# Attention with a SoLU layer on one core: small steps of three engines given out one by one

## Chip, cores and metric

The kernel runs on one core of one Trainium2 chip. The metric is device time in microseconds (us), the median of several runs. An engine is named as in the profile: PE is TensorE (matmuls), PEld its weight loads, DVE is VectorE, ACT is ScalarE, POOL is GpSimd, SP issues the DMAs.

## What is computed

For 8 batches of 8 heads, 576 positions and 64 columns per head, causal attention with a decay that is a running sum of log f; then a layer on the 4608 rows of 512 columns that come out: a product with w_in (512 x 1024), SoLU, a layer norm over 1024 columns and a product with w_out (1024 x 512).

```python
scores = scale * np.matmul(q, k.transpose(0, 1, 3, 2))
cum = np.cumsum(np.log(np.clip(f, 0.0001, 1.0)), axis=-1)
scores = np.where(causal, -1e9, scores + cum[:, :, :, None] - cum[:, :, None, :])
attn = np.exp(scores - np.max(scores, axis=-1, keepdims=True))
attn = attn / (np.sum(attn, axis=-1, keepdims=True) + 1e-09)
x = np.matmul(attn, v)                    # then heads side by side: (4608, 512)
h = x @ w_in
e = np.exp(h - np.max(h, axis=-1, keepdims=True))
solu = h * (e / (np.sum(e, axis=-1, keepdims=True) + 1e-09))
ln = (solu - mu) / np.sqrt(var + 1e-06) * g_ln
out = ln @ w_out
```

## The kernel before

**Pairs.** Attention goes by pairs of heads: 8 batches of 4 pairs. A pair's 576 queries are cut into five tiles (64, 128, 128, 128, 128 rows), and tile i sees 64 + 128 i keys. Per tile and head: PE makes the scores in a PSUM bank (lines 847, and 843 or 845 for the decay); one DVE instruction adds the mask, finds the extreme of a row and, for the larger tiles, writes the scores to SBUF (L868); ACT takes the exponential with its row sums (L873); a column step on POOL turns the sums into what is inverted (L879, tile `sm`), DVE inverts it (L880, `ri`). Then a scaled copy makes the float16 upper half of the probabilities (`copied`, printed as L527 when ACT does it and as L529 for DVE or POOL; tiles `p16s` and `wo_p`), and DVE makes the lower half (L901). A transposing DMA turns them, and PE multiplies with the values (L947). A copy out of PSUM makes the upper half of x (L962, `x_h`), DVE the lower half (L963).

**The first batch** is exact: its probabilities are scaled in float32 in place (L529, tile `p`, on POOL), turned on PE (L920), copied out of PSUM (`t_p`), and multiplied in float32 (L942).

**Layer.** Every 128 rows of x are one of 36 layer steps: product with w_in (L987, into `hps`), row maximum on DVE (L996), exponential on ACT (L998), weighing on DVE (L1002), sum of squares on ACT (L1010), five column steps on POOL (L1005 to L1007, L1013, L1014, tile `st`), normalising on POOL (L1018, tile `e`), an upper half (ACT, L527, `z<-e`), a lower half (POOL, L1023), a transposing DMA, product with w_out (L1052), a scaled copy out of PSUM on ACT (L1084, `y`), and the DMA out. Every product in float16 is three: upper by upper, upper by lower, lower by upper. PE runs them as two halves of 64 columns side by side where the order permits.

**Preparation.** w_in and w_out are read as pairs of words, put together on ACT, POOL and DVE (L608 to L644), and scaled by powers of two that come from their largest value: DVE finds it per row (L651, `top_wi`), PE turns the column (L667), DVE makes the factor, and PE spreads it over the partitions (L692). The same is done per batch for q, k and v (tiles `top`, `scale`); there ACT's squares (L709) give the size.

**Order.** The order of all engines is written out: `Plan.op` records an operation with its engine, its planned duration `ns`, what it reads and writes, and whether it uses the SBUF port that DVE and POOL share (`port`); the tuple `ORDER` gives the numbers of the 3766 operations, and `schedule` deals them out to the engines in that order, with planned start times. From these planned times comes one thing more: where the plan leaves PE idle for over 200 ns in the first 60 us, lines 1173 to 1178 put in matmuls on the identity that write into a free PSUM bank and are read by nobody ("fillers" here; 0.85 of the idle time up to 13.5 us, 0.75 up to 60 us, constant `FILLED`).

## Time and profile before

| | |
|---|---|
| three runs | 634.25, 632.65, 632.1 us; median 632.65 us |
| profiled execution | 632.48 us, of which 630.8 us span from first to last instruction |
| PE busy | 614.6 us (97%), 7852 instructions |
| DVE busy | 540.5 us (86%), 1647 instructions |
| ACT busy | 513.4 us (81%), 1295 instructions |
| POOL busy | 415.1 us (66%), 663 instructions |
| granted TensorE clock, mean | 1.000 |

A busy engine is one that has an instruction under way. A matmul's own duration contains its way through the array, so two matmuls that follow each other overlap in the table of rows; how fast PE goes is read from start to start. An idle time in brackets stands before the row that it precedes, with what ended it.

### The profile page before, as it was taken

The numbers are of one execution on the slowest core, as the hardware profiler recorded it, in microseconds if no ns is written. First come the engines' busy times: TensorE is split into PE (matmuls) and PEld (weight loads), VectorE is DVE, ScalarE is ACT, GpSimd is POOL, SyncE is SP. The second block draws the span as 40 slices with busy tenths as digits, with TensorE's granted clock in tenths as the row PEclk, the third lists the DMA queues.
The fourth block names the chain that finished last, engine by engine and source line by source line (L and its number), as shares of the span: only waits on it lengthen the run. The fifth ranks groups of instructions, "written<-read, shape, count | busy, mean of one in ns | idle before, by whom it ended". The sixth has DMA issues, their size and how long they took to land.

```text
span 630.8 us, 20471 instructions
## 1 busy us (share of the span) xinstructions
PE 614.6 (97%) x7852; PEld 362.5 (57%) x7852; DVE 540.5 (86%) x1647; ACT 513.4 (81%) x1295; POOL 415.1 (66%) x663
## 2 busy tenths in 40 slices
PE   5899999999999999999999999999999999999997
PEld 4566665565555656556565655565655655655555
DVE  6888999999999999999999998999999888774321
ACT  6798979989988997989999888899797878765342
POOL 6786761576868745878679868674777753748440
PEclk9999999999999999999999999999999999999999
DMA  8846318989999999999999999899798884876641
GB/s 331 290 153 261 122 58 178 198 165 222 205 169 190 174 230 163 214 152 254 181 201 157 257 178 261 172 169 211 126 146 149 138 167 86 155 132 126 131 118 50
DMA packets 262722, 110.99 MB, mean 176 GB/s; under 512 B 248288, under 2 KB 248736, under 8 KB 261600
## 3 DMA queue, kind: packets, MB, share of 16 engines
q1 hardware_dynamic: 262624, 109.69, 84.1%
q8 instruction: 61, 1.00, 0.7%
q14 instruction: 37, 0.30, 0.1%
HBM read 38.27 MB, written 9.66 MB: 76 GB/s over the span
## 4 chain that ended last, share of the span: by engine, by line
PE 78%; DVE 10%; DMA 5%; ACT 4%; issue 2%; POOL 2%; SPq 1%; DVEq 0%; POOLq 0%; ACTq 0%
PE ps L1052 26%; PE hps L987 25%; PE ps L847 10%; PE ps L947 10%; PE ps L845 3%; DVE p L868 2%; DMA wo_raw<-in_w_in_dram 2%; PE ps L920 1%; DMA zz<-z 1%; DVE wo_p L901 1%; DVE st L996 1%; DVE p16s L901 1%; DMA t_p<-wo_p 1%; PE ps L942 1%; DMA t_raw<-in_w_out_dram 1%
## 5 line engine op out<-in xcount | busy, mean ns | idle before, releaser
L1052 PE MATMUL ps<-wo_f,zz 128*64 128x512 f16 (+1 forms) x1599 | 196.2, 380 | 0.6 <-DMA zz<-z 0.6
L873 ACT ACTIVATE p<-p,nm 128x320 f32<-128x320 f32 (+4 forms) x208 | 133.0, 641 | 13.3 <-DVE nm L868 12.1
L1052 PEld LDWEIGHTS <-zz 128*64 128x64 f16 (+1 forms) x1599 | 90.5, 109 | 84.5 <-issue 7.1
L987 PE MATMUL hps<-wi_h,x_h 128*64 128x512 f16 (+1 forms) x564 | 111.4, 383 | 0.2
L987 PE MATMUL hps<-wi_l,x_h 128*64 128x512 f16 (+1 forms) x564 | 110.2, 379 | 0.0
L987 PE MATMUL hps<-wi_h,x_l 128*64 128x512 f16 (+1 forms) x564 | 110.2, 379 | 0.0
L868 DVE CUSTOM_DVE_ANT_0 p<-ps,mask 128x320 f32<-128x320 f32 (+3 forms) x208 | 99.5, 496 | 6.7 <-PE ps L920 2.4
L847 PE MATMUL ps<-qk 64*128 64x288 f16 (+9 forms) x1056 | 100.7, 303 | 1.8 <-DMA qk<-in_qk_dram 1.0
L879 POOL TENSOR_SCALAR sm<-sm 128x2 f32<-128x2 f32 (+1 forms) x128 | 39.7, 310 | 85.0 <-ACT p L873 53.1
L987 PEld LDWEIGHTS <-x_h 128*64 128x64 f16 (+1 forms) x1128 | 59.8, 109 | 59.1 <-issue 14.7
L1023 POOL TENSOR_TENSOR z<-e,z 128x512 f16<-128x512 f32 x64 | 77.2, 1220 | 24.7 <-ACT z L527 23.9
L901 DVE SCALAR_TENSOR_TENSOR wo_p<-p,ri,wo_p 128x448 f16<-128x448 f32 (+1 forms) x112 | 85.5, 778 | 7.5 <-ACT wo_p L527 6.8
L947 PEld LDWEIGHTS <-v 128*64 128x64 f16 x2520 | 72.8, 110 | 10.5 <-issue 2.7
L947 PE MATMUL ps<-t_p,v 128*64 128x128 f16 (+1 forms) x2520 | 76.3, 218 | 0.1
L996 DVE TENSOR_REDUCE st<-hps 128x1 f32<-128x1024 f32 x36 | 43.8, 1216 | 18.8 <-PE hps L987 18.6
L529 POOL TENSOR_SCALAR wo_p<-p,ri 128x576 f16<-128x576 f32 x56 | 46.5, 834 | 11.3 <-DVE ri L880 9.7
L998 ACT ACTIVATE e<-hps,st,unscale 128x1024 f32<-128x1024 f32 x32 | 38.4, 1201 | 16.2 <-DVE st L997 12.4
L1002 DVE SCALAR_TENSOR_TENSOR e<-hps,e 128x1024 f32<-128x1024 f32 x36 | 43.7, 1214 | 9.0 <-ACT e L998 8.8
L847 PEld LDWEIGHTS <-qk 64*128 64x128 f16 x864 | 32.4, 94 | 32.4 <-issue 21.6
L845 PE MATMUL ps<-crow,pick 64*128 64x448 bf16 (+1 forms) x360 | 50.9, 276 | 0.0
L1010 ACT ACTIVATE junk<-e,st 128x1024 bf16<-128x1024 f32 x36 | 41.2, 1145 | 11.6 <-DVE e L1002 10.0
L987 PEld LDWEIGHTS <-x_l 128*64 128x64 f16 (+1 forms) x564 | 32.6, 110 | 29.6
(188 smaller groups left out, 1176.7 us busy)
## 6 DMA issues: line engine op xcount, KB each, us to landing
raws<-in_qk_dram SPq DMA_DIRECT2D x24, 576.0 KB, 5.8
vraw<-in_v_dram SPq DMA_DIRECT2D x8, 1280.0 KB, 7.1
out_dram<-y SPq DMA_DIRECT2D x35, 256.0 KB, 3.2
qk<-in_qk_dram SPq DMA_DIRECT2D x8, 576.0 KB, 6.4
wo_raw<-in_w_in_dram SPq DMA_DIRECT2D x4, 1024.0 KB, 8.6
vraw<-in_w_out_dram SPq DMA_DIRECT2D x2, 1024.0 KB, 4.9
t_raw<-in_w_out_dram SPq DMA_DIRECT2D x2, 1024.0 KB, 5.0
t_p<-p16s SPq DMA_TRANSPOSE x84, 3.5
```

What stands on the lines that cost most here:

```text
L529: (nc.vector if eng == DVE else nc.gpsimd).tensor_scalar(now(out_), now(in_), scale, by, ALU.mult, ALU.mult)
L845: nc.tensor.matmul(dst, pick[row(h), a2, a1:a1 + 1].broadcast_to([D, P]), crow[row(h), a2, cols], start=False, stop=True)
L847: nc.tensor.matmul(dst, x[row(h), 0, q0:q0 + P], y[row(h), 1, cols], start=(n == 0), stop=False)
L868: op(DVE, R_NS[i] if n == 0 else 442, at[i][h] + STEPS[0], lambda i=i, h=h, n=n, a=a, e=e, x=x, m0=m0: nc.vector.tensor_tensor_reduce(home ...
L873: op(ACT, E_NS[i] + (0 if banked(p, i) or i == 4 else 28), at[i][h] + STEPS[1], lambda i=i, h=h, x=x: nc.scalar.activation(home(i, h), hom ...
L901: op(DVE, L_NS[j], at[j][g] + STEPS[4], lambda j=j, g=g, nq=nq, h16=h16, l16=l16, r1=r1: nc.vector.scalar_tensor_tensor(l16(), home(j, g, ...
L947: nc.tensor.matmul(o[row(h), a:a + n], v16[m][:, x, 2 * j + h], t[:, y, i + j if h else i - j], start=(j == 0 and c == 0), stop=(j == i an ...
L987: nc.tensor.matmul(hps[k, sl], x[:, k], w[:, c, sl], start=start, stop=stop)
L996: op(DVE, 1215, at, lambda: nc.vector.tensor_reduce(s[:, 0:1], hps, axis=AX.X, op=ALU.max, negate=True), [("h",)], [("st", n % 2)])
L1002: nc.vector.scalar_tensor_tensor(et, hps, 1.0 / DFF, et, ALU.mult, ALU.mult, accum_out=s[:, 3:4])
L1023: op(POOL, 1085, at, lambda a=a: nc.gpsimd.tensor_tensor(z16[:, a, 1], e2[:, a], z16[:, a, 0], ALU.subtract), [ek, zk_], [(*zk_, "l", a)])
L1052: nc.tensor.matmul(y[t], zz[:, a, x, j][:, t], wo(w, k), start=(k == 0 and n == 0), stop=(k == NFC - 1 and n == 2))
```

## The change

Operations that could run on several engines are no longer bound by class. `Plan.op` takes `either`, a table of engines with planned durations, and looks its own number up in a new table `ON`: 83 numbers for ACT, 151 for DVE, 57 for POOL; an operation that is in none keeps the engine of its class. The tuple `ORDER` is a new permutation of the same 3766 numbers. No other constant differs.

```diff
+        o.either, o.may = either, port
+        if either:
+            eng, given = next((e for e in either if len(self.ops) in ON.get(e, ())), eng), fn
+            ns, port = either[eng], port and eng == DVE
+
+            def fn():
+                given(o.eng)
...
+ON = {
+    ACT: {
+        83, 91, 92, 113, 128, 129, 181, 217, 380, 384, 416, 420, 422, 424, 440, 450, 452, 454, 456, 460, 490, 492, 496, 652, 1040, 1103, 1113, 1115,
...
     def copied(eng, ns, due, out_, in_, reads, writes, scale=1.0, clear=(), port=True, by=1.0):
 
-        def fn():
-            if eng == ACT:
+        def fn(e):
+            if e == ACT:
                 nc.scalar.activation(now(out_), now(in_), AF.Copy, scale=scale)
             else:
-                (nc.vector if eng == DVE else nc.gpsimd).tensor_scalar(now(out_), now(in_), scale, by, ALU.mult, ALU.mult)
-        op(eng, ns[eng], due, fn, reads, writes, clear=clear, port=port and eng == DVE)
+                engine(e).tensor_scalar(now(out_), now(in_), scale, by, ALU.mult, ALU.mult)
+        either = ns if by == 1.0 else {e: x for e, x in ns.items() if e != ACT}
+        op(eng, ns[eng], due, fn, reads, writes, clear=clear, port=port, either=either)
...
-        op(POOL, 310, at[i][1] + STEPS[2], lambda: nc.gpsimd.tensor_scalar(sums, sums, 1.0e-9, 1.0 / P_UP, ALU.add, ALU.mult), sk, [("se", m, i)])
+        op(POOL, 310, at[i][1] + STEPS[2], lambda e: engine(e).tensor_scalar(sums, sums, 1.0e-9, 1.0 if p < NFP * NPAIR else 1.0 / P_UP, ALU.add, ALU.mult), sk, [("se", m, i)], port=True, either={POOL: 310, DVE: 67})
...
-                copied(P_SCALE[j], {POOL: N_NS[j], ACT: 187 + 0.83 * w, DVE: 67 + 0.6 * w}, at[j][g] + STEPS[3], *[lambda j=j, g=g, nq=nq: home(j, g, nq)] * 2,
-                       [("ri", m, j), ("p", j)], [("p", j, g)], scale=ri[m][:nq, j, g:g + 1], by=1.0 / P_UP)
+                copied(P_SCALE[j], {POOL: N_NS[j], ACT: 187 + 0.83 * w, DVE: 117 + 0.6 * w}, at[j][g] + STEPS[3], *[lambda j=j, g=g, nq=nq: home(j, g, nq)] * 2,
+                       [("ri", m, j), ("p", j)], [("p", j, g)], scale=ri[m][:nq, j, g:g + 1])
...
-            op(ACT, 68 + 0.83 * w, at + XSTEP[0], lambda xo=xo, key=key, w=w: nc.scalar.activation(xo[0], ps[plan.place[key]][:, :w], AF.Copy, scale=up), [key, *uk], xk)
+            copied(ACT, {ACT: 68 + 0.83 * w, DVE: (122 if exact else 72) + 1.05 * w}, at + XSTEP[0], xo[0], lambda key=key, w=w: ps[plan.place[key]][:, :w], [key, *uk], xk, scale=up, port=False)
```

In the same way `either` is given to two memsets, two steps of the running sum, the backwards copy of it, the upper half of v, four of the layer's five column steps, the normalising, the lower half of z and the copy of y. For the first batch the factor 1 / P_UP is no longer taken in both the column step and the scaling, so that ACT, which multiplies by one factor, can do the scaling too.

Counted in the built programs, by kind (before, then now):

| kind | before | now |
|---|---|---|
| column step on the sums (`sm`) | POOL 128 | POOL 92, DVE 36 |
| column steps of the layer (`st`; L1005, L1006, L1007, L1013) | POOL 144 | POOL 105, DVE 39 |
| scaling of the first batch's `p` | POOL 40 | POOL 23, ACT 9, DVE 8 |
| upper half of the probabilities, larger tiles (`wo_p`) | ACT 56, POOL 56 | ACT 58, POOL 50, DVE 4 |
| the same, 320 columns, from SBUF (`p16s`) | ACT 56 | ACT 29, POOL 23, DVE 4 |
| the same, from PSUM, 64 and 192 columns (`p16s`) | ACT 112 | ACT 93, DVE 19 |
| `x_h` | ACT 72 | ACT 56, DVE 16 |
| upper half of q and k (`qk`) | POOL 48 | POOL 22, ACT 25, DVE 1 |
| upper half of v | POOL 28 | POOL 16, ACT 12 |
| upper half of z | ACT 32 | ACT 21, POOL 8, DVE 3 |
| lower half of z (L1023) | POOL 64 | POOL 58, DVE 6 |
| normalising in place (L1018) | POOL 32 | POOL 28, DVE 4 |
| copy of y | ACT 35 | ACT 31, DVE 4 |
| first batch's turned probabilities (`t_p`) | DVE 20, ACT 16 | DVE 11, ACT 25 |
| fillers on PE | 91 | 69 |

The order at three places follows; line numbers of the changed kernel are some 29 higher from `copied` on (L920 is now L949, L667 L696, L692 L721, L947 L976, L1178 L1207, L879 L908, L529 L558, L527 L556).

PE before, from the spreading of w_in's factor on (`scale_wi`; `p_63` to `p_65` are the first pair's probabilities, `ident` the identity; of the fillers one stands):

```order
L920 MATMUL ps_150<-ident,p_63 128x64
L692 MATMUL ps_146<-scale_wi,ones 128x2
L1178 LDWEIGHTS ident
L1178 MATMUL ps_150<-ident 128x256
...
L920 MATMUL ps_150<-ident,p_65 128x128 x3
L920 MATMUL ps_149<-ident,p_65 128x128 x2
L847 MATMUL ps_145<-qk_1_71 128x320
L847 MATMUL ps_146<-qk_1_71 128x320
...
L942 MATMUL ps_150<-t_0_p,vraw_76 64x128 x6
L920 MATMUL ps_149<-ident,p_64 128x128 x3
L1178 LDWEIGHTS ident
L1178 MATMUL hps<-ident 128x256
```

and now:

```order
L949 MATMUL ps_150<-ident,p_63 128x64
L721 MATMUL ps_147<-scale_wi,ones 128x2
L949 MATMUL ps_150<-ident,p_64 128x128 x3
L949 MATMUL ps_149<-ident,p_65 128x128 x2
L949 MATMUL ps_147<-ident,p_65 128x128 x3
L1207 LDWEIGHTS ident
L1207 MATMUL ps_150<-ident 128x256
...
L971 MATMUL ps_150<-t_0_p,vraw_76 64x64 x2
L971 MATMUL ps_150<-t_0_p,vraw_76 64x128 x4
L876 MATMUL ps_145<-qk_1_71 128x320
L876 MATMUL ps_149<-qk_1_71 128x320
```

The first pair's transposes now stand together, with the pair's first values right behind them and ahead of the second pair's scores. The fillers from here to the end of the stretch are 35 before (4, 6, 4, 10, 4, 1, 5, 1) and 14 now (5, 2, 1, 1, 2, 3); ahead of it they are 56 and 55.

POOL before, where the first pair's `p` are scaled:

```order
L879 TENSOR_SCALAR sm_93<-sm_93 128x4
L529 TENSOR_SCALAR p_63<-p_63,ri_89 64x64
L529 TENSOR_SCALAR p_64<-p_64,ri_89 128x192
L611 TENSOR_SCALAR wo_raw<-wo_raw 128x1024
L879 TENSOR_SCALAR sm_93<-sm_93 128x2
...
L529 TENSOR_SCALAR p_65<-p_65,ri_89 128x320 x2
L529 TENSOR_SCALAR p_64<-p_64,ri_89 128x192
L529 TENSOR_SCALAR wi_h<-z_105,scale_wi 128x1024
```

and now on POOL:

```order
L908 TENSOR_SCALAR sm_93<-sm_93 128x4
L640 TENSOR_SCALAR wo_raw<-wo_raw 128x1024
L558 TENSOR_SCALAR p_64<-p_64,ri_89 128x192
L558 TENSOR_SCALAR p_63<-p_63,ri_89 64x64
L558 TENSOR_SCALAR p_64<-p_64,ri_89 128x192
L558 TENSOR_SCALAR wi_h<-e_103,scale_wi 128x1024
```

Of the pair's six scalings POOL keeps three; one `p_63` and both `p_65` are ACT's, and the second `sm_93` step is DVE's.

PE before, at the factor of the third batch (`top_113` is turned, `scale_119` is spread):

```order
L667 MATMUL ps_145<-ident,top_113 1x128 x3
L847 MATMUL ps_148<-qk_2_72 128x448
L847 MATMUL ps_150<-qk_2_72 128x448
...
L692 MATMUL ps_145<-scale_119,ones 128x6
L947 LDWEIGHTS v_0_79
L947 MATMUL ps_147<-t_0_p,v_0_79 64x64
```

and now:

```order
L696 MATMUL ps_150<-ident,top_113 1x128 x3
L976 LDWEIGHTS v_0_79
L976 MATMUL ps_147<-t_0_p,v_0_79 64x64
...
L876 MATMUL ps_145<-qk_2_72 128x448
L876 MATMUL ps_149<-qk_2_72 128x448
...
L721 MATMUL ps_150<-scale_119,ones 128x6
```

36 products with the values of the fifth pair now stand between the turning and the spreading; before, all 90 came behind it. Over the whole program PE changes the shape of its array (tile size of a matmul against that of the one before) 243 times before and 248 times now.

## Rows read from the trace of the kernel before

**Rows 1.** The page: busy time by engine, and the granted clock in 40 slices.
```profile
PE 614.6 (97%) x7852; PEld 362.5 (57%) x7852; DVE 540.5 (86%) x1647; ACT 513.4 (81%) x1295; POOL 415.1 (66%) x663
...
PEclk9999999999999999999999999999999999999999
```

**Rows 2.** Busy time by stretch: stretch, length, busy us (count) of each engine.
```profile
18.30:61.00 42.70, 40.76 (x413) 26.82 (x413) 36.91 (x123) 37.48 (x106) 32.37 (x50) 1.00 0.61 216
...
100.00:320.00 220.00, 217.31 (x2984) 126.08 (x2982) 212.56 (x682) 199.33 (x521) 150.75 (x233) 1.00 1.03 197
320.00:500.00 180.00, 180.00 (x2459) 103.56 (x2455) 166.97 (x506) 155.96 (x400) 130.57 (x199) 1.00 0.97 178
...
560.00:630.80 70.80, 67.55 (x739) 39.20 (x733) 24.49 (x47) 29.32 (x49) 31.08 (x50) 1.00 0.48 107
```

**Rows 3.** Timeline of PE at 309 us: start, length, instructions.
```profile
309.46 0.38 PE L987 MATMUL hps<-wi_l,x_h 128*64 128x512 f16 x2
309.68 0.38 PE L987 MATMUL hps<-wi_h,x_l 128*64 128x512 f16 x2
309.99 0.26 PE L847 MATMUL ps<-qk 64*128 64x64 f16 x6
```

**Rows 4.** Busy time by stretch, of the fillers (L1178) alone.
```profile
18.30:61.00 42.70, 5.17 (x35) 3.18 (x35) 1.00 0.61 216
```

**Rows 5.** Timeline of PE, 25 to 41 us; idle time before a row in brackets.
```profile
25.27 0.27 PE L667 MATMUL ps<-ident,top 128*1 128x128 f32 x1 [0.59 <-DVE top L662]
...
34.56 1.26 PE L1178 MATMUL hps<-ident 128*128 128x256 bf16 x10
35.98 0.77 PE L920 MATMUL ps<-ident,p 128*128 128x128 f32 x5 [0.15 <-POOL p L529]
36.58 0.60 PE L1178 MATMUL hps<-ident 128*128 128x256 bf16 x4
37.34 0.52 PE L920 MATMUL ps<-ident,p 128*128 128x128 f32 x3 [0.16 <-POOL p L529]
...
40.34 0.41 PE L987 MATMUL hps<-wi_h,x_h 128*64 128x512 f16 x2
```

**Rows 6.** Waits of PE over the whole span: total us, times, longest.
```profile
PE ps L667 <- DVE top_wi L662: 1.4, 1, 1.4
...
PE ps L692 <- DVE scale L690: 0.9, 1, 0.9
...
PE ps L920 <- POOL p L529: 0.8, 4, 0.2
```

**Rows 7.** Timeline of PE at 114 us.
```profile
113.99 0.36 PE L845 MATMUL ps<-crow,pick 64*128 64x448 bf16 x2
115.23 0.38 PE L692 MATMUL ps<-scale,ones 1*128 1x6 f32 x2 [0.89 <-DVE scale L690]
```

**Rows 8.** The chain that ended last, in order of time: start, length.
```profile
143.63 0.95 PE ps L947 x36
```

**Rows 9.** Groups of DVE by line and shape: busy us, mean ns of one.
```profile
L963 DVE SCALAR_TENSOR_TENSOR x_l<-ps,x_h 128x256 f16<-128x256 f32 x28 | 11.6, 413 | 7.5 <-ACT x_h L962 7.3
L529 DVE TENSOR_SCALAR t_p<-ps 128x384 f32<-128x384 f32 x16 | 8.5, 548 | 0.3 <-PE ps L920 0.3
L997 DVE TENSOR_SCALAR st<-st,unscale 128x1 f32<-128x1 f32 x32 | 6.8, 211 | 0.7
...
L529 DVE TENSOR_SCALAR wi_h<-e,scale_wi 128x1024 f16<-128x1024 f32 x2 | 1.5, 728 | 0.0
...
L698 DVE TENSOR_SCALAR scale<-ps 128x3 f32<-128x3 f32 x6 | 0.9, 147 | 0.0
```

**Rows 10.** Groups of POOL by line and shape, as in the group before.
```profile
L529 POOL TENSOR_SCALAR wo_p<-p,ri 128x576 f16<-128x576 f32 x56 | 46.5, 834 | 11.3 <-DVE ri L880 9.7
...
L529 POOL TENSOR_SCALAR wi_h<-z,scale_wi 128x1024 f16<-128x1024 f32 x2 | 4.9, 2464 | 0.7 <-DVE z L628 0.7
```

**Rows 11.** Timeline of POOL at 21 us.
```profile
21.56 3.81 POOL L529 TENSOR_SCALAR wi_h<-z,scale_wi 128x1024 f16<-128x1024 f32 x1 [0.65 <-DVE z L628]
```

More of the change, by code (lines that the diff above doesn't have):

```diff
@@ L81 @@
 class Op:
-    __slots__ = ("eng", "ns", "fn", "deps", "users", "take", "keys", "left", "ready", "end", "tail", "seq", "dense", "port", "form", "layer", "blocks", "hold", "forms")
+    __slots__ = ("eng", "ns", "fn", "deps", "users", "take", "keys", "left", "ready", "end", "tail", "seq", "dense", "port", "form", "layer", "blocks", "hold", "forms", "either", "may")
 class Plan:
@@ L253 @@
 STAGES = (39.55, 3.04, -33.03, 23.93, 18.38)
-ORDER = (
[149 rows of a table removed]
+ON = {
+    ACT: {
[4 rows of a table added]
+    },
+    DVE: {
[7 rows of a table added]
+    },
+    POOL: {
[3 rows of a table added]
+    },
+}
+ORDER = (
[149 rows of a table added]
 )
@@ L455, in tile_kernel @@
     pick = sb("pick", 2, 4 * NPAIR, dtype=BF16)
-    op(POOL, 700, -70, lambda: nc.gpsimd.memset(crow, 0.0), writes=[("crow0",)])
+    op(POOL, 1060, -70, lambda e: engine(e).memset(crow, 0.0), writes=[("crow0",)], port=True, either={POOL: 1060, DVE: 540})
     def picks():
@@ L545, in tile_kernel @@
         dma(-100, ft[D * h:D * h + D], f.rearrange("b h s -> (b h) s"), 144, writes=[("fraw", 1) if h else ("e", 0)])
-    op(POOL, 800, -99, lambda: nc.gpsimd.memset(zero, 0.0), writes=[("z", 0)])
+    op(POOL, 580, -99, lambda e: engine(e).memset(zero, 0.0), writes=[("z", 0)], port=True, either={POOL: 580, DVE: 540})
     op(DVE, 70, -100, lambda: nc.vector.memset(nhalf, 1.0), writes=[("table0",)])
@@ L1016, in layer @@
         if turned:
-            op(c_eng, {POOL: 1165, DVE: 690}[c_eng], at, lambda: engine(c_eng).tensor_scalar(et, et, s[:, 4:5], s[:, 7:8], ALU.add, ALU.mult),
-               [("st6", n % 2), ("st7", n % 2)], [ek], port=c_eng == DVE)
+            op(c_eng, 0, at, lambda e: engine(e).tensor_scalar(et, et, s[:, 4:5], s[:, 7:8], ALU.add, ALU.mult),
+               [("st6", n % 2), ("st7", n % 2)], [ek], port=True, either={POOL: 1165, DVE: 690})
             e2 = et.rearrange("p (a n) -> p a n", a=2)
@@ L1022, in layer @@
             for a in range(2):
-                op(POOL, 1085, at, lambda a=a: nc.gpsimd.tensor_tensor(z16[:, a, 1], e2[:, a], z16[:, a, 0], ALU.subtract), [ek, zk_], [(*zk_, "l", a)])
+                op(POOL, 1085, at, lambda e, a=a: engine(e).tensor_tensor(z16[:, a, 1], e2[:, a], z16[:, a, 0], ALU.subtract), [ek, zk_], [(*zk_, "l", a)],
+                   port=True, either={POOL: 1085, DVE: 610})
         else:
@@ L1083, in layer @@
         at += tout
-        op(ACT, 590, at, lambda: nc.scalar.activation(yt, ps[plan.place[key]], AF.Copy, scale=us[:, 2:3]),
-           [key, *yu], [yk])
+        copied(ACT, {ACT: 590, DVE: 660}, at, yt, lambda: ps[plan.place[key]], [key, *yu], [yk], scale=us[:, 2:3], port=False)
         dma(at, out[n * P:(n + 1) * P, :], yt, 256, reads=[yk])
```

27 lines of the change are left out of this document (13 added, 14 removed), and 311 rows, old and new, of tables (ON, ORDER).

## Prediction

> **What bounds the kernel now.** I read the page first. PE is busy for 614.6 of 630.8 us, and the clock that it is granted is full in all 40 slices [rows 1]; since a busy PE need not be a fast one, the next view is the timeline. In the layer products one pair of half-width products of 512 columns starts 0.22 us behind the other (309.46, 309.68), which is 512 columns at 2.4 GHz, and the only thing that breaks the stream there is a change of the array's shape: the next start is 0.31 us on (309.68, 309.99), so about 0.1 us for each change [rows 3]. From 320 to 500 us PE is never without work [rows 2]. So PE is the bound, and what a change of the other three engines can give is what PE loses. Three views show that: the waits of PE, the fillers, and the timeline around them. In the stretch from 18.3 to 61 us PE loses most: 35 fillers take 5.2 us [rows 4], and several end in a wait: 0.59 us for a maximum, 0.15 and 0.16 us for the first batch's scaled probabilities [rows 5]. Later the longest wait for an engine is 0.9 us, for the factor of the third batch [rows 6].
>
> DVE comes next: from 100 to 500 us it is busy for 212.56 + 166.97 of 400 us, so 20.5 us are idle [rows 2]. From 560 us on it works for 24.5 of 70.8 us [rows 2]; what is added there is hidden beside layer products.
>
> **The change part by part.** The products themselves are the same. The sum is made against the profiled execution, 632.48 us (span 630.8 and 1.7 around it), which is 0.17 us under the median of 632.65; the terms are carried to the median.
>
> *The first 18.3 us: 0.* The fillers there are 56 and now 55, and the stretch ends when DVE has the largest value of w_in (1.4 us of wait [rows 6]). That work stays on DVE in nearly the same order. Two memsets go from POOL to DVE ahead of it, where DVE waits for its first DMA anyway.
>
> *18.3 to 61 us: -2.3 us and -0.8 us.* The order has 14 fillers where 35 stood. One takes 0.11 us from start to start (ten take 1.26 us, the last 0.27 of which is its way through the array [rows 5]), so 21 fewer are 2.3 us, if the work that they waited for does come earlier. There is a reason for it to: before, all of the first batch's scalings were POOL's, one after the other, and POOL was held up: one upper half of w_in took 3.81 us [rows 11], while the mean of two is 2.46 [rows 10], so the other took 1.12. Now 9 of the 40 scalings are ACT's and 8 DVE's, and of four upper halves of w_in, one is ACT's, none DVE's. PE's four waits for these scalings, 0.8 us in all [rows 6], go as well: I count the whole of it. Bounds of the two together: nothing (the fillers go, the idle time stays, since the last to come is a DMA or the squares on ACT, behind which ACT's new scalings queue) and 6.1 us (all 5.2 us of fillers and the 0.9 us of waits in rows 5). I take 3.1, near the middle: it is what the fillers' own row gives.
>
> *The third batch's factor: -0.9 us.* PE stands from the end of its scores to 115.23 us for it [rows 7]. Now 36 products with values stand between the turning of the maxima and the spreading of the factor; 36 such take 0.95 us elsewhere [rows 8]. That covers the wait, if the fifth pair's transposing DMA has landed some 4 us sooner than it is now needed; it had no wait to spare in these rows, so the bounds are 0 and -0.9.
>
> *Shape changes: +0.5 us.* 248 instead of 243, at 0.1 us [rows 3].
>
> *DVE's new work: 0, with a price.* Counted up to the 32nd layer maximum in DVE's order (which is near 560 us), it gets 61 column steps at 0.15 to 0.21 us (the two rows of such steps [rows 9]), 9 to 13 us; 36 copies out of PSUM, mostly of 64 to 320 columns, of which a step of 256 takes 0.41 us [rows 9], some 13 us; 16 scalings from SBUF at 0.71 ns a column (728 ns for 1024 [rows 9]), 4 us; and two memsets. It loses 12 copies of turned probabilities (0.55 us for 384 columns [rows 9]), two halves of w_in (0.73 us) and two subtractions, some 9 us. Net 18 to 22 us over 560 us; spread evenly, 400/560 of 20 us or 14 us fall between 100 and 500 us, where 20.5 us are idle. It fits, barely, and some of that idle time is waiting for the very copies that DVE now makes itself: the group of 256 columns alone waited 7.3 us for ACT's upper half [rows 9]. I take 0. Bounds: -1 (shorter chains of copies) and what the second rival gives.
>
> *POOL and ACT: 0.* POOL loses work and is idle a third of the span [rows 1]; ACT's count hardly changes.
>
> Sum: -2.3 - 0.8 - 0.9 + 0.5 = -3.5 us. From the profiled execution that gives 629.0, from the median **629.2 us**, 0.55% faster. About 0.3%, or 1.9 us, is what a measurement can tell from no change: faster is under 630.75, slower over 634.55.
>
> **The rivals.**
>
> *Nothing to see, 632.0 us.* The fillers are only put where the planned times leave PE idle. That the plan sees less idle time is a plan's opinion; where the work comes no earlier, PE stands still instead of running fillers. For it: the longest waits in the stretch are for a maximum that comes off ACT's squares and for w_in's largest value, and ACT gets three scalings ahead of the squares. Against it: the two waits for POOL in rows 5, and that PE now has a product with w_in and more values of the first batch to do where ten fillers stood. Then only the third batch's wait and the shape changes count: 632.65 - 0.9 + 0.5 = 632.25, and a little of the waits for POOL, so 632.0.
>
> *Slower, 637.6 us: DVE becomes the bound between 100 and 500 us.* The place is the attention of batches 3 to 7, where DVE is busy for 95% of the time. The price: 14 us of steps, and a port. POOL's 3.81 us for what else takes 1.12 shows one of the two engines standing while the other uses SBUF [rows 10, 11]; the wait can fall on either. If each of the 16 new SBUF scalings of DVE stands for half of a POOL scaling (0.834 us [rows 10], so 0.42), that is 6.7 us. Together 20.7 us, against 20.5 us of idle time. It decides from the point where the idle time can't be filled: if all of it can, 0.2 us is over; if half can, 10.4. The middle is 5.0 us, and as PE then waits for scores and upper halves, what it gained at the start is lost with them: 632.65 + 5.0 = 637.6. Against it: DVE's own waits for ACT's copies go, POOL's share of the port shrinks, and PE's order has layer products between the pairs.
> The Trainium skill speaks for this rival (SBUF — State Buffer, "SBUF: two separate sides"): the port pair that VectorE and GpSimd share is an exclusive lock, kept for a whole instruction by whichever started first, while the other blocks completely. By that rule every one of these 16 scalings can stand behind a whole POOL instruction, and the time would be that of this rival; the one long row of POOL agrees with the rule, and the busy times of DVE show no sign yet that it decides.
>
> *All idle time of the start goes, 625.6 us.* If both bounds of the second term and the third are reached, -6.1 - 0.9, the sum is 625.65. For it: three engines instead of one feed PE's transposes. Against it: the waits for maxima have chains of their own on DVE, which stay.
>
> **How the numbers follow.** Forecast 0.56, nothing to see 0.20, DVE bound 0.15, all idle time gone 0.09. The forecast's own range is 627.0 to 631.5. The range from 625.0 to 635.5 takes in the bounds of the starting stretch, the whole of the second case, and the lower part of DVE's case; half of the latter and a few per cent below are left out. Faster: nearly all of the forecast and the last case, 0.62. Same: a little of the forecast, and the second case, 0.22. Slower: 0.16.
>
> **What would show it.** Right: fewer fillers, the first layer product ahead of its 40.34 us [rows 5], the wait for the third batch's factor gone, layer products at 0.22 us as before, and DVE busier from 100 to 500 us, with PE busy there as much as now. Wrong: PE idle where fillers stood between 18 and 61 us (the second case); or new waits of PE for `nm`, `p16s` or transposing DMAs after 100 us, with DVE at 98% or more (the third); or a wait of PE at the values of the fifth pair, which now come sooner.

## The result

The change makes the kernel slower: 638.94 us, the median of 6 runs (637.64 to 639.48), against 633.01 for 6 runs of the kernel before; the ratio is 1.0091, with a 95% interval from 1.0073 to 1.0109. The forecast was 629.2 us, so the sign was wrong, and the time lies above the range of 625.0 to 635.5. The profiled execution took 637.99 us with a span of 636.3.

Lines of the changed kernel carry numbers 29 higher than before for the same statement: L868, the mask step, is L897, L901 is L930, L987 is L1016, L1023 (lower halves `z`) is L1052. In the experiments they are some lines lower or one higher, as the table `ON` is printed in fewer lines or lines are added. The page of the changed kernel, which answers to [rows 1]:

```profile
PE 616.6 (97%) x7842; PEld 365.7 (57%) x7842; DVE 574.7 (90%) x1781; ACT 512.9 (81%) x1271; POOL 360.7 (57%) x553
...
PEclk9899999999999998999999999999999999999999
```

POOL gave up 54 us and DVE took 34. The granted clock is no longer full everywhere. Busy time by stretch, as in [rows 2] (the clock stands behind POOL's column), then the fillers alone, as in [rows 4]:

```profile
18.30:61.00 42.70, 40.35 (x389) 25.51 (x389) 39.80 (x140) 38.67 (x106) 23.76 (x34) 0.96 0.55 201
100.00:320.00 220.00, 214.03 (x2873) 124.94 (x2871) 212.82 (x690) 199.69 (x514) 137.03 (x205) 0.99 0.96 189
320.00:500.00 180.00, 179.59 (x2491) 105.24 (x2487) 172.98 (x546) 157.10 (x389) 115.96 (x167) 1.00 0.98 184
560.00:636.20 76.20, 72.69 (x802) 42.01 (x796) 44.63 (x96) 26.32 (x47) 20.79 (x31) 0.99 0.57 109
```
```profile
18.30:61.00 42.70, 3.12 (x14) 1.39 (x14) 0.96 0.55 201
```

PE lost 3.3 us of busy time between 100 and 320 us (217.31 before), where DVE's busy time hardly rose (212.56 before): most of DVE's new work, 20 us of it, lies behind 560 us. Two stretches of 3.41 us have half the clock, 1.2 GHz (windows cut to them; the clock is the 0.50):

```profile
20.97:24.38 3.41, 3.41 (x25) 2.67 (x23) 3.41 (x9) 2.71 (x6) 3.08 (x3) 0.50 0.69 236
249.66:253.08 3.42, 3.42 (x70) 3.38 (x70) 3.42 (x10) 2.84 (x9) 1.27 (x3) 0.50 0.80 121
```

The waits of PE over the span, as in [rows 6]:

```profile
...
PE ps L876 <- DVE scale L727: 2.3, 1, 2.3
PE ps L976 <- DVE nm L897: 1.4, 4, 0.6
PE ps L696 <- DVE top_wi L691: 1.4, 1, 1.4
...
PE ps L949 <- POOL unscale L748: 1.1, 1, 1.1
PE ps L876 <- DVE nm L897: 0.8, 1, 0.8
PE ps L721 <- DVE scale L719: 0.7, 1, 0.7
```

The waits of 2.3, 1.1 and 0.8 us are new, and so is most of the 1.4 us for `nm`. The longest ends at 248.84 us. The scores that wait there don't read the fifth batch's factors; DVE's L727, which the profile names, reads these factors out of PSUM, so I take what the scores lack to be the bank that holds them until then. Right behind the wait comes the second fall of the clock. Timelines of PE, then of DVE and POOL ahead of it:

```profile
248.84 0.74 PE L876 MATMUL ps<-qk 64*128 64x448 f16 x6 [2.34 <-DVE scale L727]
```

```profile
244.83 2.62 DVE L930 SCALAR_TENSOR_TENSOR p16s<-p,ri,p16s 128x320 f16<-128x320 f32 x2
247.38 0.15 DVE L909 RECIPROCAL ri<-sm 128x2 f32<-128x2 f32 x1
247.45 1.20 DVE L1025 TENSOR_REDUCE st<-hps 128x1 f32<-128x1024 f32 x1
248.57 0.14 DVE L726 TENSOR_SCALAR scale<-ps 128x1 f32<-128x1 f32 x1
```
```profile
244.59 2.52 POOL L1052 TENSOR_TENSOR z<-e,z 128x512 f16<-128x512 f32 x2 [0.72 <-ACT z L556]
```

Two steps of 320 columns took 2.62 us beside POOL's two halves of `z`. In the kernel before, the same two take 1.00 us; there they start ahead of the halves (DVE, then POOL):

```profile
241.99 1.00 DVE L901 SCALAR_TENSOR_TENSOR p16s<-p,ri,p16s 128x320 f16<-128x320 f32 x2
```
```profile
242.97 2.27 POOL L1023 TENSOR_TENSOR z<-e,z 128x512 f16<-128x512 f32 x2 [1.17 <-ACT z L527]
```

In the change the row maximum (1.20 us) and then the factors queue behind them on DVE. At 181.5 us another pair of `z` halves meets two lower halves of queries and keys, and at 30.2 us a copy of POOL's meets a new scaling of DVE's (timelines again, DVE and then POOL for each place):

```profile
180.79 3.70 DVE L831 SCALAR_TENSOR_TENSOR qk<-raws,scale,qk 128x576 f16<-128x576 f32 x2
```
```profile
180.88 0.75 POOL L766 COPY unscale_(2, 3)_135<-unscale 64x2 f32<-64x2 f32 x1
181.60 2.27 POOL L1052 TENSOR_TENSOR z<-e,z 128x512 f16<-128x512 f32 x2
```
```profile
30.06 1.40 DVE L558 TENSOR_SCALAR p<-p,ri 128x192 f32<-128x192 f32 x1
31.39 0.41 DVE L558 TENSOR_SCALAR t_p<-ps 128x256 f32<-128x256 f32 x1
```
```profile
29.94 0.31 POOL L558 TENSOR_SCALAR p<-p,ri 64x64 f32<-64x64 f32 x1 [0.44 <-DVE ri L909]
30.23 1.11 POOL L558 TENSOR_SCALAR wi_h<-z,scale_wi 128x1024 f16<-128x1024 f32 x1
```

In each case POOL's long row starts within 0.25 us of DVE's (at 181 us, of the second of DVE's two steps, 181.52), and the DVE instructions that were held up are 0.7 to 2.2 us longer than the median of their shape. That is what the Trainium skill describes (SBUF — State Buffer, "SBUF: two separate sides"): one lock for both engines, held for a whole instruction by whichever came first. The traces agree: at 244.59 us POOL came first, and at 30.06 and 181.52 us an earlier instruction of POOL's was still under way (until 30.25 and 181.64), behind which the long one passed ahead of DVE too. What it costs the kernel is another matter, as the experiments show.

**Theory A**: what costs is turns at the port that DVE loses to POOL at places where PE waits for DVE, and the falls of the clock behind such waits. **Theory B**, the second rival of the prediction: DVE has too much to do.

To see where time is lost, the table gives how far each kernel's PE is behind the kernel before (us, negative: ahead). It is worked out from the starts of all matmuls but the fillers, as the difference of the times at which the same share of all columns has been started; a product that uses half of the array counts half. The head of a column is the time in the kernel before. The kernels with the change's order can be compared with each other to 0.1 us. Against the kernel before, whose order differs, a value inside the span holds only to about 1 us; at 615 us it agrees with the difference of the spans to 0.3 us. The experiments' rows are used below.

| kernel | 23 us | 62 us | 156 us | 203 us | 225 us | 248 us | 424 us | 615 us |
|---|---|---|---|---|---|---|---|---|
| the change | 2.2 | 0.7 | -0.7 | 0.2 | 2.0 | 4.8 | 5.4 | 5.2 |
| e11, one turn | 3.4 | 2.0 | 0.6 | 1.4 | 3.2 | 6.1 | 6.6 | 6.3 |
| e1, turns | 1.5 | 0.4 | -0.9 | -0.2 | 1.7 | 1.3 | 1.7 | 1.5 |
| e2, fillers | 1.1 | 1.4 | 0.3 | 2.2 | 4.0 | 6.5 | 7.4 | 7.1 |
| e5, third turn | 0.8 | -0.7 | -2.1 | -1.4 | 0.4 | 0.0 | 0.5 | 0.2 |
| e12, four steps | 0.7 | -1.5 | -2.9 | -2.1 | -2.0 | -2.4 | -1.9 | -2.1 |
| e16, four steps alone | 2.4 | 1.4 | 0.0 | 0.9 | 1.1 | 2.4 | 2.9 | 2.6 |
| e8, steps alone | 0.3 | -0.2 | -0.8 | -1.1 | -0.4 | -1.3 | -0.9 | 1.8 |

So the change is not behind all along: it is 2.2 us behind around its first fall of the clock and 0.7 at 62 us, is level or ahead at 156, and loses 2.7 us between 156 and 225 us and 2.8 between 225 and 248.

### The profile page after: what moved, and what is told of

The parts are those of the page before. It is cut to its first block, busy times and chain, and to the rows that moved or that the text cites. A ratio compares the mean times of both kernels' runs of the same rounds, so it can differ in the third digit from the quotient of the medians.

```text
span 636.3 us, 20454 instructions
## 1 busy us (share of the span) xinstructions
PE 616.6 (97%) x7842; PEld 365.7 (57%) x7842; DVE 574.7 (90%) x1781; ACT 512.9 (81%) x1271; POOL 360.7 (57%) x553
## 4 chain that ended last, share of the span: by engine, by line
PE 54%; DVE 6%; POOL 2%; issue 1%; ACT 0%; DVEq 0%; POOLq 0%
PE ps L1082 19%; PE hps L1016 19%; PE ps L976 7%; PE ps L876 5%; PE ps L874 2%; DVE p16s L930 1%; DVE p L897 1%; POOL z L1052 1%; DVE qk L831 1%; DVE wo_p L930 1%; DVE st L1025 0%; DVE e L1031 0%; DVE x_l L992 0%; PE ps L1096 0%; PE ps L1099 0%
## 5 line engine op out<-in xcount | busy, mean ns | idle before, releaser
L902 ACT ACTIVATE p<-p,nm 128x448 f32<-128x448 f32 (+4 forms) x208 | 133.3, 644 | 21.2 <-DVE nm L897 21.1
L1016 PE MATMUL hps<-wi_h,x_h 128*64 128x512 f16 (+1 forms) x563 | 111.7, 383 | 0.4 <-DVE e L1031 0.4
L1016 PE MATMUL hps<-wi_l,x_h 128*64 128x512 f16 (+1 forms) x563 | 110.5, 379 | 0.0
L1016 PE MATMUL hps<-wi_h,x_l 128*64 128x512 f16 (+1 forms) x563 | 110.5, 379 | 0.0
L897 DVE CUSTOM_DVE_ANT_0 p<-ps,mask 128x320 f32<-128x320 f32 (+4 forms) x208 | 100.0, 497 | 6.6 <-PE ps L874 2.9
L1016 PEld LDWEIGHTS <-x_h 128*64 128x64 f16 (+1 forms) x1126 | 60.6, 109 | 58.8 <-issue 14.6
L930 DVE SCALAR_TENSOR_TENSOR wo_p<-p,ri,wo_p 128x448 f16<-128x448 f32 (+1 forms) x112 | 87.9, 800 | 1.1 <-POOL wo_p L558 1.0
L1052 POOL TENSOR_TENSOR z<-e,z 128x512 f16<-128x512 f32 x58 | 69.9, 1214 | 29.2 <-ACT z L556 23.5
L976 PEld LDWEIGHTS <-v 128*64 128x64 f16 x2520 | 74.5, 112 | 11.7 <-issue 4.2
L976 PE MATMUL ps<-t_p,v 128*64 128x128 f16 (+1 forms) x2520 | 77.7, 220 | 1.4 <-DVE nm L897 1.4
L908 POOL TENSOR_SCALAR sm<-sm 128x2 f32<-128x2 f32 (+1 forms) x92 | 28.8, 313 | 85.7 <-ACT p L902 64.4
L558 POOL TENSOR_SCALAR wo_p<-p,ri 128x576 f16<-128x576 f32 (+1 forms) x50 | 41.0, 823 | 34.3 <-DVE ri L909 25.4
L874 PE MATMUL ps<-crow,pick 64*128 64x448 bf16 (+1 forms) x360 | 50.7, 276 | 0.0
L1016 PEld LDWEIGHTS <-x_l 128*64 128x64 f16 (+1 forms) x563 | 32.9, 110 | 29.3
```

Source lines behind the costliest of these rows:

```text
L874: nc.tensor.matmul(dst, pick[row(h), a2, a1:a1 + 1].broadcast_to([D, P]), crow[row(h), a2, cols], start=False, stop=True)
L897: op(DVE, R_NS[i] if n == 0 else 442, at[i][h] + STEPS[0], lambda i=i, h=h, n=n, a=a, e=e, x=x, m0=m0: nc.vector.tensor_tensor_reduce(home ...
L902: op(ACT, E_NS[i] + (0 if banked(p, i) or i == 4 else 28), at[i][h] + STEPS[1], lambda i=i, h=h, x=x: nc.scalar.activation(home(i, h), hom ...
L930: op(DVE, L_NS[j], at[j][g] + STEPS[4], lambda j=j, g=g, nq=nq, h16=h16, l16=l16, r1=r1: nc.vector.scalar_tensor_tensor(l16(), home(j, g, ...
L976: nc.tensor.matmul(o[row(h), a:a + n], v16[m][:, x, 2 * j + h], t[:, y, i + j if h else i - j], start=(j == 0 and c == 0), stop=(j == i an ...
L1016: nc.tensor.matmul(hps[k, sl], x[:, k], w[:, c, sl], start=start, stop=stop)
```

## The experiments

Every run in one table: median, ratio to runs of the kernel before on the same chip with its 95% interval, and in how many of the executions the mean granted clock was under 0.9985 (one fall of 3.41 us to half makes 0.997 of a span like this).

| run | median us | ratio | clock fell in |
|---|---|---|---|
| the change | 638.94 | 1.0091 (1.0073 to 1.0109) | 6 of 6 |
| e1_turns | 635.44 | 1.0039 (1.0023 to 1.0056) | 11 of 12 |
| e2_fillers | 638.94 | 1.0095 (1.0075 to 1.0114) | 6 of 6 |
| e3_turns_fillers | 634.19 | 1.0020 (1.0001 to 1.0039) | 5 of 12 |
| e4_before_unfilled | 631.92 | 0.9994 (0.9980 to 1.0009) | 3 of 12 |
| e5_third_turn | 633.21 | 1.0010 (0.9994 to 1.0027) | 6 of 12 |
| e6_fourth_turn | 634.88 | 1.0030 (1.0013 to 1.0046) | 6 of 12 |
| e7_steps_back | 636.51 | 1.0054 (1.0034 to 1.0074) | 9 of 9 |
| e8_steps_alone | 634.63 | 1.0041 (1.0022 to 1.0059) | 2 of 12 |
| e9_early_steps | 633.19 | 1.0001 (0.9984 to 1.0019) | 5 of 12 |
| e10_turns_no_steps | 631.85 | 0.9986 (0.9975 to 0.9998) | 9 of 12 |
| e11_one_turn | 638.55 | 1.0084 (1.0062 to 1.0106) | 6 of 6 |
| e12_four_steps | 630.30 | 0.9955 (0.9938 to 0.9972) | 2 of 7 |
| e13_held_clock | 631.41 | 0.9973 (0.9963 to 0.9984) | 0 of 12 |
| e14_before_held | 631.40 | 0.9970 (0.9957 to 0.9983) | 1 of 12 |
| e15_best | 630.52 | 0.9962 (0.9949 to 0.9975) | 0 of 7 |
| e16_four_steps_alone | 635.75 | 1.0043 (1.0027 to 1.0059) | 6 of 8 |

The kernel before, over all its 122 executions beside these: 631.96 us in the median of the 70 whose clock did not fall, 633.09 for 41 with a mean of 0.996 or 0.997 (one fall), 635.12 for 11 with less.

### e1 to e4: the turns and the clock

**e1_turns**: three places in DVE's part of the order, four operations moved (numbers of operations; other engines' numbers left out). 1477 is a lower half of queries and keys, 1579 and 1580 are the two steps of 320 columns, 1942 are the fifth batch's factors.

```diff
-1475, 1477, 1209, 1191, 1208,
+1475, 1209, 1191, 1208, 1477,
...
-1599, 1602, 1570, 1600, 1580, 1579, 1594, 1365, 1942,
+1599, 1580, 1579, 1602, 1570, 1600, 1594, 1942, 1365,
```

> The changed kernel with three VectorE steps of its order put elsewhere: the second lower half of queries and keys (pair 12) behind the three score masks that follow it, the two lower halves of 320 columns (pair 13) ahead of the mask step before them, and the scale factors of the fifth batch ahead of the row maximum. Theory A (two turns at the shared port lost to GpSimd's pair of z products, at 181.5 and 244.8 us, cost TensorE 2.1 and 3.3 us, the second with its fall of the clock): these go, 633.5 us (632.5 to 635), no fall of the clock near 250 us. Theory B (VectorE simply has too much to do from 100 to 500 us, 34 us more than before in the whole): what is gained there is lost at other places, 637.5 to 639.

635.44 us, just above the expected range; by the ratio, 0.52% of the loss of 0.91% is gone. The two steps of 320 columns now take 1.01 us, the factors come at 245.44, and PE's wait of 2.3 us and the fall behind it are gone (DVE):

```profile
243.24 1.01 DVE L925 SCALAR_TENSOR_TENSOR p16s<-p,ri,p16s 128x320 f16<-128x320 f32 x2
245.44 0.14 DVE L721 TENSOR_SCALAR scale<-ps 128x1 f32<-128x1 f32 x1
245.57 1.21 DVE L1020 TENSOR_REDUCE st<-hps 128x1 f32<-128x1024 f32 x1
```

By the table the gain at this place is 3.2 us: between 225 and 248 us the change lost 2.8, e1 gains 0.4. DVE does the same work in both kernels. Two things were moved here at once, though, and no run parts them: the steps came out of POOL's way, and the factors came ahead of a row maximum of 1.2 us. With the port alone put right, the factors would have come 1.6 us sooner than in the change, and PE would still have stood for some 0.7 us (an estimate from these rows).

**e11_one_turn**, run later, moves only the step at 181.5 us (the first of the two pieces).

> The changed kernel with the turn at 181.5 us alone put right (one lower half of queries and keys behind the three masks that follow it). Theory A by the trace's course: 2.1 us of the 5.4, so 636.8 us (636 to 637.5), and the wait at 246 us with its fall of the clock stays. Theory B: 638 to 639.5.

638.55 us, in theory B's range, and no gain beyond the interval. DVE's step takes 1.26 us there instead of 3.0, and PE's wait of 0.8 us is gone, yet from 156 to 203 us PE falls behind by 0.8 us as it did in the change (0.9). My price of 2.1 us for this turn was wrong: nothing of it shows. So what e1 gained, it gained at the place at 244.8 us.

**e2_fillers** and **e3_turns_fillers** add fillers into `hps`, to the change and to e1 (49 is the transpose for w_in's largest value, 95 a transpose of the first pair):

```diff
+HOLD_PE = {49: 8, 95: 4}
...
+            for _ in range(HOLD_PE.get(o.seq, 0)):
+                nc.tensor.matmul(hps[:, :256], blank[:, :P], blank, start=True, stop=True)
             o.fn()
```

> The changed kernel with 12 fillers more: 8 while TensorE waits for the topmost weight (17.2 to 18.6 us) and 4 ahead of the transposes at 20.7 us. Theory A: the first fall of the clock (21.0 to 24.4 us) goes, which cost half of 3.41 us, against 0.4 us of fillers on the path: 637.5 us (637.0 to 638.0). If TensorE's pace there is set by VectorE and GpSimd anyway (theory B, or the rival that nothing is to be seen at the start): 638.7 to 639.4, with or without the fall.

> The three moved VectorE steps and the 12 fillers together. Theory A: the gains add, 632.2 us (631 to 634), that is no slower than the kernel before, and a granted clock of 1.00 throughout. Theory B: 637 to 639.

e2: 638.94, no gain, though in its profile the early fall is gone and PE is only 1.1 us behind at 23 us instead of 2.2. At 62 us it is 1.4 behind, twice as much as the change: its ACT stood for the second load of w_out (1.96 us idle up to 50.7 us), and PE 1.3 us for ACT; that load took 6.8 us to land after 4.7 in the change. e3: 634.19, a ratio of 1.0020, so the expected 631 to 634 was missed, and the clock still fell in 5 of 12 executions. Its interval and e1's overlap: that the gains add is not shown.

**e4_before_unfilled** leaves out the 4 fillers of the kernel before at 20.4 us.

> The kernel before without the 4 fillers at 20.4 us. If these alone keep the clock up there: it falls at about 21 us for some 3.4 us and the time is 633.0 + 1.7 - 0.4 = 634.3 us (633.8 to 635). If they do nothing: 632.6 us, clock 1.00.

631.92 us, the same as before. Its profiled execution has a fall at 20.39 us, but only 3 of 12 executions have one at all, and 11 of 29 of the kernel before beside them: those 4 fillers are not what holds the clock.

### e5 to e8: a third and a fourth turn, and theory B by itself

**e5_third_turn**: e1, and in POOL's part of the order the copy (201) behind the two unscale steps (61).

```diff
-201, 61,
+61, 201,
```

> The three moved VectorE steps, and GpSimd's copy of the input weights' fourth block (1.11 us at 30.2 us) put behind its two small unscale steps. At 30.06 us VectorE's scaling of 192 columns stood 1.40 us for that copy, its copy of a transposed tile behind it came 1 us later, and TensorE stood 1.1 us at 30.6 to 31.9 us for the bank, ahead of the last score products that read the running sums and so release the buffer of the output weights' load. Theory A: that wait goes, the load is issued about 1 us earlier than at 34.4 us, and the time is 1 us below the kernel with the three moved steps: 633.5 us (632.8 to 634.3). Theory B (VectorE full): no gain, 634 to 635.

633.21 us: with the same work on every engine as in the change, the kernel is level with the one before. PE's wait of 1.1 us has shrunk to 0.3. The profile of the change put it down to POOL's `unscale`, on which those transposes don't depend; as I read it, the bank that they need is freed by DVE's copy at 31.39 us, right behind the scaling that stood for the port. How much of the 1.8 us between the medians of e1 and e5 this turn is worth, is open. The intervals overlap, e1's clock fell in 11 of 12 executions and e5's in 6, and the fall in e1's profile is at 12 us, ahead of the moved copy; in the table e1 is 0.7 us behind e5 at 23 us already and 1.1 at 62. SP issues the first load of w_out into `t_raw` 2.15 us earlier than in the change (timelines of SP: the kernel before, the change, e5):

```profile
33.21 10.51 SPq L533 DMA_DIRECT2D t_raw<-in_w_out_dram  x2
```
```profile
34.93 10.29 SPq L563 DMA_DIRECT2D t_raw<-in_w_out_dram  x2
```
```profile
32.78 10.27 SPq L558 DMA_DIRECT2D t_raw<-in_w_out_dram  x2
```

This load goes into the buffer of the running sums, which the last near score products (L843, in the change L872) read; SP waits for them, and ACT and POOL read what was loaded.

**e6_fourth_turn**: e5, and around 198 us the row maximum, two probability steps and a mask step ahead of one lower half.

```diff
-1619, 1548, 1235, 997, 1269, 1234, 998, 1270, 1298,
+1619, 997, 998, 1235, 1234, 1269, 1270, 1298, 1548,
```

> As the last, and around 198 us of VectorE's order the row maximum, two steps on probabilities and the mask step behind them put ahead of one lower half of queries and keys, which with its neighbours stood 1.8 us for GpSimd's z products there. Theory A: the waits of TensorE at 204 to 220 us (0.7, 0.5 and 0.5 us) shrink by half or more, another 1 us: 632.5 us (631.5 to 633.7). Theory B: no gain, 634 to 635.

634.88 us, worse than e5. The steps that I put later feed a transposing DMA, and PE now stood 1.95 us at 223 us for `t_p<-p16s`. The miss shows what this move cost, not which turn to give up.

**e7_steps_back**: the change, with the 36 steps on the sums of probabilities (L908) given back to POOL.

```diff
 ON = {DVE: {
-    89, 135, 365, 447, 629, 641, 1088, 1198, 1230, 1269, 1301, 1664, 1703, 1717, 1735, 2032, 2064, 2103,
-    2147, 2439, 2608, 2622, 2910, 2951, 3079, 3111, 3123, 3314, 3342, 3426, 3440, 3561, 3573, 3619, 3631, 3660,
```

> The changed kernel with the 36 sums-of-columns steps (0.15 us each) given back from VectorE to GpSimd, all else as in the change. Theory B (VectorE full): VectorE has 36 x 0.08 = 2.9 us less to do and the time falls by 1 to 3 us, to 636 to 638. Theory A (it is the turns that cost, not the sum of the work): no gain, 638.5 to 641, since GpSimd's port time moves by 36 x 0.3 us and the turns at 181.5 and 244.8 us stay lost.

636.51 us. Here theory B foresaw the number and theory A did not. **e8_steps_alone** is the other side: the kernel before with these 36 on DVE.

> The kernel before (its order and its engines), with those 36 steps alone given to VectorE. Theory A: an order made for other engines keeps its won turns: within 0.3% of the kernel before, 631 to 634. Theory B: 2.9 us more on VectorE, slower by 1 to 3 us, 633 to 635.

634.63 us, again as theory B had it. But where the time went is not what B says. Up to 450 us e8 is ahead of the kernel before by 0.9 us, with 23 of the 36 steps done; it loses 2.6 us between 450 and 532 us, where PE waits 0.9 us for the transposing DMA of `z` and 0.4 us for a step of DVE's; the rest is not resolved. Busy time from 460 to 535 us (columns as in [rows 2]) of the kernel before, of e8, and of e5, where all of the change's work is on DVE:

```profile
460.00:535.00 75.00, 75.00 (x1032) 43.39 (x1030) 67.01 (x204) 62.20 (x170) 47.34 (x77) 1.00 0.77 136
```
```profile
460.00:535.00 75.00, 73.58 (x1014) 43.39 (x1014) 69.58 (x207) 60.28 (x165) 46.16 (x69) 1.00 0.75 135
```
```profile
460.00:535.00 75.00, 75.00 (x1033) 43.56 (x1030) 70.75 (x224) 59.37 (x158) 47.30 (x68) 1.00 0.86 144
```

DVE is at least as busy in e5 (70.75 against 69.58 us, part of which is that e8 got less done in these 75 us), and PE stands for nothing there. So the sum on DVE is not what stops PE at this place: two orders with the same steps on DVE differ in what PE waits for.

### e9, e10, e12, e16: which steps

**e9_early_steps**: e8 with only the 23 steps ahead of 440 us.

> The kernel before with only the 23 of the 36 steps that stand before 440 us given to VectorE (the run with all 36 lost its 3 us between 469 and 532 us and was 1.2 us ahead until 460). Theory A (what costs is where a step stands): no loss at 469 to 532 us, 630.8 us (630 to 632.5). Theory B (VectorE full): 23/36 of the loss of the run with all, 2.4 us x 0.64 = 1.5 us, that is 633.5 us (633 to 634.5).

633.19 us: as a time this lies in theory B's range, but the kernel before was at 632.68 beside it, and the ratio of 1.0001 (0.9984 to 1.0019) shows no loss; B's 1.5 us would have been 1.0024. So these 23 steps cost nothing that can be told, and e8's loss belongs to the 13 behind 440 us.

**e10_turns_no_steps**: e5 and e7 together.

> The changed kernel with its three turns put right (as in the third-turn run, 633.2 us) and the 36 steps back on GpSimd. Theory B: a further 2.4 us, 630.8 us (630 to 631.8). Theory A: what the steps' return won in the changed kernel was a part of the turn at 244.8 us, which is right here already: 632.5 to 634.5 us.

631.85 us, 0.24% under e5 (the intervals just overlap) and between the two theories' numbers, which points to a cost of the steps apart from the three turns. PE's waits for `nm` at 204 and 220 us were gone in it, which pointed to four steps.

**e12_four_steps**: e5 with four numbers taken out of `ON`.

```diff
 ON = {DVE: {
-    1198, 1230, 1269, 1301,
```

> As the third-turn run (633.2 us), with only four of the 36 steps given back to GpSimd: those between 181 and 205 us. Theory A (where a step stands decides): these four carry the gain of all 36, 631.9 us (631.3 to 632.6), and TensorE's waits at 190 to 220 us shrink from 2.3 to about 0.8 us. Theory B (the sum of VectorE's work): 4/36 of 1.4 us, no measurable gain, 632.8 to 633.5.

630.30 us: 0.55% under e5, more than all 36 gave, and 0.45% under the kernel before. Four steps of 0.15 us, and between 156 and 225 us PE loses 0.9 us instead of 2.5. What one of them does is seen at 199 us. In e5, DVE and then POOL:

```profile
199.67 1.57 DVE L925 SCALAR_TENSOR_TENSOR wo_p<-p,ri,wo_p 128x448 f16<-128x448 f32 x1
201.16 1.21 DVE L1020 TENSOR_REDUCE st<-hps 128x1 f32<-128x1024 f32 x1
202.30 0.15 DVE L903 TENSOR_SCALAR sm<-sm 128x4 f32<-128x4 f32 x1
```
```profile
198.46 0.60 POOL L761 COPY unscale_(2, 3)_135<-unscale 64x2 f32<-64x2 f32 x1
199.14 1.62 POOL L1047 TENSOR_TENSOR z<-e,z 128x512 f16<-128x512 f32 x1
```

In e12, the same:

```profile
198.98 0.67 DVE L924 SCALAR_TENSOR_TENSOR wo_p<-p,ri,wo_p 128x448 f16<-128x448 f32 x1
199.58 1.21 DVE L1019 TENSOR_REDUCE st<-hps 128x1 f32<-128x1024 f32 x1
```
```profile
198.50 0.60 POOL L760 COPY unscale_(2, 3)_135<-unscale 64x2 f32<-64x2 f32 x1
199.54 0.20 POOL L902 TENSOR_SCALAR sm<-sm 128x4 f32<-128x4 f32 x1 [0.44 <-ACT ps L896]
199.82 1.16 POOL L1046 TENSOR_TENSOR z<-e,z 128x512 f16<-128x512 f32 x1
```

On POOL the step stands between the two halves of `z` and waits for ACT; it holds the second half back until 199.82, and DVE's lower half of 448 columns has passed by then, in 0.67 us instead of 1.57. The row maximum behind it starts 1.58 us sooner than in e5, where DVE was 0.69 us later already. Moved to DVE, the step no longer separates the halves. The same rows show a second effect: the step itself is done at 199.54 us on POOL and only at 202.30 on DVE, where it stands behind the row maximum, so what it feeds comes later. No run parts the two, and for the other three steps neither is shown. Either way it is the step's place that counts and not its 0.15 us.

**e16_four_steps_alone**: the change without those four steps on DVE, and nothing else.

> The changed kernel with nothing but the four steps between 181 and 205 us given back to GpSimd. Theory A with the places adding: the 2 us that they are worth between 192 and 225 us, the turns at 30 and 244.8 us staying lost: 637 us (636 to 638). If a step less moves the later turn too, as it may have with all 36 given back (636.5 us): 634.5 to 636. Theory B: 638.5 to 639.5.

635.75 us, 0.48% less than the change, about what the four were worth in e5. That is below theory A's range and in that of the alternative, but not for its reason: in the profile the turn at 245 us is still lost (2.62 us for the two steps, 2.3 us of wait), but no fall of the clock followed it in that execution. This gives a price for the fall: between 225 and 248 us e16 loses 1.3 us, the change with the same wait and the fall 2.8.

### e13 to e15: holding the clock

**e13_held_clock** and **e14_before_held** put fillers into the waits of the first 21 us: 20 into e10, 16 into the kernel before (69 is the first score product). **e15_best** puts the 20 into e12.

```diff
+HOLD_PE = {69: 8, 49: 8, 95: 4}
```

In e14 the last entry is left out.

> The three turns put right, the 36 steps back on GpSimd (631.85 us), and 20 fillers: 8 ahead of the first score product (10.4 us), 8 ahead of the transpose of the topmost weight (17.2 us), 4 ahead of the transposes at 20.7 us. If early falls of the clock cost time: the executions without a fall become the rule and the median goes to that of the former run's undisturbed executions, 630.7 us (630.2 to 631.3). If they cost nothing in the end: 631.8 to 632.4 us.

> The kernel before with 16 of the same fillers (ahead of the first score product and of the transpose of the topmost weight). If early falls cost time: the third of its executions that has one loses it, median 632.0 us against 632.4 (631.5 to 632.4). Otherwise the same as before, 632.3 to 633.

> The third-turn run's order, the four steps of 181 to 205 us on GpSimd, and the 20 fillers of the first 21 us. If the gains add: no fall of the clock before the end, 629.6 us (629.0 to 630.3), 0.5% under the kernel before. If the fillers, which stand on TensorE's path in part, cost what they give here: 630.2 to 631.

With them the clock fell in 1 of 31 executions; in e3, which lacks the 8 ahead of the first score product, it fell in 5 of 12. e14 is 0.30% under the kernel before, by 16 matmuls in time that was idle. Among the executions without a fall it is still 0.12% (631.38 us against 632.14 beside it); why, is open. In e13 they gave 0.13% (0.9986 to 0.9973, with overlapping intervals), where the three executions of e10 without a fall (630.74 us in the median) had promised 0.18%; e15 is not better than e12 (the intervals overlap), so there the gains don't add. e12 and e15 are both faster than the kernel before and than the change.

## Why the prediction was wrong

**The bound** was read rightly: PE, and what the others give is what PE loses. The changed kernel loses in waits of PE and in its clock, and e12 gains by removing them.

**18.3 to 61 us, -3.1: mis-sized, and its gain was lost again.** The fillers went as counted, 14 for 35, and took 3.12 us for 5.17, though five of the 14 ran at half the clock. At 20.1 and at 60.0 us the kernels have started the same products, so this stretch can be read without the table: the change is 0.3 us behind at the first and 0.6 at the second, so it lost 0.3 us where 3.1 were to be won. Half the clock for 3.41 us is up to 1.7 us of that. PE's waits for POOL's scalings also made way for one of 1.07 us behind DVE's scaling at the port, of which some 0.4 us is left at 60 us (e1 against e5). e5 and e12, with that turn put right and no fall, win 1.4 and 1.8 us between the same points: that is what the term was worth, about half of 3.1. Of the four waits for scalings that the term counted, three with 0.6 us lie in this stretch. The first layer product did come early (36.02 us, before 40.34 [rows 5]), which shows how little that says. In the change itself the first rival, nothing to see, was the nearer one for this stretch, though not for its reason.

**Third batch's factor, -0.9: mis-sized.** The wait went from 0.89 [rows 7] to 0.74 us:

```profile
115.24 0.38 PE L721 MATMUL ps<-scale,ones 1*128 1x6 f32 x2 [0.74 <-DVE scale L719]
```

The term took the factor's time for given by PE's turning of the maxima. PE did turn them 0.5 us sooner (111.81 against 112.31 us), but DVE's chain of steps to the factor starts at 113.12 us and ends at 115.18 in both kernels, since five masks stand ahead of it now and not two. With the smaller waits beside it, PE stands for 0.9 us there instead of 1.5.

**DVE's new work, 0: failed, and this is the step that gave the wrong sign.** The term asked whether the sum fits into DVE's idle time. It does, better than I thought: 6.3 us more between 100 and 500 us (385.8 for 379.5), not 14. But the price is not in the sum. With all of that work left on DVE, four moved operations of DVE's and one moved copy of POOL's bring back 0.81% of the 0.91% (e1, e5; part of the latter may be fewer early falls of the clock), and four steps of 0.15 us are worth 0.5% (e12, e16).

**The rival "DVE becomes the bound", 637.6 us,** came close in time and named the right port and the right neighbours, but its mechanism, a sum of 20.7 us against 20.5 us, is refuted by e5 (the same work, level with before) and by the stretch from 460 to 535 us; DVE was busy for 96% from 100 to 500 us, not for the 98% that the prediction gave as its sign. Its middle was also added up wrongly: between 0.2 and 10.4 it is 5.3 us and not 5.0, which gives 638.0. That this is so near the measured time is luck. Its price per new scaling, 0.42 us, was an average over 16; in fact a few steps paid 0.7 to 2.2 us each, of which only the one at 30 us is a new scaling, the others being lower halves that DVE had before too. And only those on PE's path counted: the one at 181.5 us cost nothing that e11 could find.

**POOL, 0: failed by omission.** I counted POOL's lost work as harmless. e12 shows a place where a POOL step that went away had kept a port instruction back.

**The clock** stood in no term. In the kernel before one fall goes with 1.1 us more (631.96 to 633.09), and five of the six executions of the change had a mean clock that means two or more.

The loss by places: at 615 us the change is 7.3 us behind e12, in which the turns and the four steps are put right. Of these, 3.2 us come between 225 and 248 us (about 1.5 of them the fall, by e16), 1.8 between 156 and 225 us (1.6 by e12 against e5: the four steps), 0.7 between 23 and 62 us, where the turn at 30 us lies (but where e5 and e12, which run the same program up to 181 us, differ by 0.7 as well), and 1.5 ahead of 23 us, where the change's clock fell and e12's did not. The kernel before stands between the two, 2.1 us behind e12: so much the change wins once these are put right. Open remains why the medians give the four steps 3 us where the profiles give 1.6. Falls of the clock are not the reason: among the executions without one, e5 is 0.8 us above and e12 2.1 us under the kernel before on the same chip. Open is also which turns e8 loses behind 450 us; they were not tried apart.

## What to carry to other kernels

When two engines share a port and both run in a fixed order, cost a moved step by what it meets and what it stops holding back, not by its duration: look at what the neighbour starts within 0.3 us of each port instruction, and at which of these the bounding engine waits. Where fewer fillers are counted as a gain, compare the two kernels at points where both have started the same products, with the fillers left out, and look up which DMA the stretch needs (e2 stood for one). A wait of the bounding engine can cost a second time through the clock (1.3 us without the fall, 2.8 with it).
